# Row 0's mean from two scaled sums, its first weight slice on two queues, and row 1 turned sooner

## The chip, the cores and the metric

One core of one Trainium2 chip. The metric is device microseconds of one execution; the kernel before takes 503.67 us (median of 3 runs, 503.43 to 503.75).

## The reference, cut to what matters

```python
xn = _layernorm(x)                       # x: 1 x 2048 x 576, bf16; eps 1e-5, no scale or shift
return x + _A_ref(xn, A_wqkv, A_wo) + _B_ref(xn, B_w_gate, B_w_up, B_w_down)

# A: dilated local attention, 32 heads of 18, each position looks at 8 keys, 2 apart
qkv = xn @ wqkv                          # 576 -> 1728
logits = einsum(q, k[pos - 2 * w]) * scale, w = 0..7; attn = softmax(logits)
o = einsum(attn, v[pos - 2 * w]) @ wo
# B: SwiGLU, 576 -> 4608 -> 576
(silu(xn @ w_gate) * (xn @ w_up)) @ w_down
```

## The kernel before, in words

The 2048 positions lie as 16 rows of 128: partition p holds positions 16p to 16p + 15, and "row r" is one position of each partition, a tile of 128 x 576. The first 60 us normalize the rows and compute QKV row by row; then four turns of 512 positions follow, each with nine chunks of the gate and up projections (L601) and the down projection (L630), while VectorE computes the attention beside them. The change touches the first 16 us only.

A matmul needs a row with its 576 columns on the partitions, so each normalized row is turned in five slices of 128 columns (the last holds columns 512 to 575 twice, the copy being the "pad"). Rows 0 and 1 are turned on TensorE with 128 x 128 transposes into PSUM (`transp_pe`, L258) and copied to SBUF (`copy_pt`, L267); rows 2 to 4 with half transposes (`transp_halves`, L274), whose two halves ScalarE and VectorE copy (L287); rows 5 and up by DMA transposes. The weights of QKV (576 x 1728) lie as four slices of 128 rows (`load_w`, L147: slices 0 to 3, 432 KB each) and a rest of 64 rows in two DMAs.

Row 0 is treated apart, since everything waits for it. VectorE takes mean and variance (`ln_stats`, two `bn_stats` of 288 columns at L214 and a `bn_aggr` at L218), subtracts the mean only (`ln_center`, L248; GpSimd does the pad, L253), and the centered row is turned and multiplied. Its rstd (`ln_sqrt` on ScalarE, L226, then `ln_recip` on VectorE, L231) is multiplied in where row 0's results leave PSUM (`p_evac`, L345). The fully normalized row 0 (`ln_apply`, L236) is made as well, for the later projections, and turned by a DMA transpose.

The order on every engine is the order of the calls in the program, written by hand (L477 to L551); engines run in order and wait for each other by semaphores that the tile layer places. Ahead of row 0, ten matmuls of 512 columns and one of 128 on constants (`warm_pe`, L171) keep TensorE busy. Then row 0 is turned; QKV row 0 begins with slices 0, 1 and half of 2 (`p_whole`, L304); between its matmuls row 1's transposes stand, in three PSUM tiles (`pt1`, `pa`, `pb`); then slice 0 of row 1, slice 3 and the rest of row 0; then `p_row(1)`, with row 2's half transposes inside it at the place (0, 2), that is, in its second pass behind slice 2 of the first group pair; then `p_row(2)`. PSUM has 8 tiles in rotation: four results of row 0, four of row 1; row 2's half transposes take over the first two of row 0's.

Loads go out on two queues: ScalarE's (x row 0, weight slice 1) and SP's (x row 1, slice 0, slice 2, x row 2, slice 3, the rest, x row 3, then the other 12 rows in three DMAs). Eight DMA semaphores are used in turn, so a DMA's issue waits until the eighth DMA before it has landed.

Of the kernel before, what the change touches and what calls it, by code (L numbers as in the profile page):

```python
# [9 lines left out]
bf16 = mybir.dt.bfloat16  # L10
f32 = mybir.dt.float32
ACT = mybir.ActivationFunctionType
ALU = mybir.AluOpType
# [4 lines left out]
P = 128  # L18
H, DH, W, DIL = 32, 18, 8, 2
D = H * DH  # L20
HALF = D // 2
G = 432
# [3 lines left out]
DPAD = KT * P  # L26
# [44 lines left out]
def kernel(  # L71
# [11 lines left out]
    nc = tc.nc  # L83
# [6 lines left out]
    x_v = A_x.rearrange("b (p r) d -> p (b r) d", r=R)  # L90
    out_v = out.rearrange("b (p r) d -> p (b r) d", r=R)

    const = ctx.enter_context(tc.tile_pool(name="const", bufs=1))
# [19 lines left out]
    PP = big.tile([P, 2, RT * D], bf16, name="PP")  # L113
# [8 lines left out]
    wdf = wd[:].rearrange("p f j -> p (f j)")  # L122
    XC, XN = RT * D, RT * DPAD
    xc_b = [wdf[:, i * XC:(i + 1) * XC].rearrange("p (r d) -> p r d", d=D) for i in range(4)]
# [4 lines left out]
    wqkv = hTf[:, 0:12 * D].rearrange("p (k j) -> p k j", j=3 * D)  # L129
# [14 lines left out]
    def load_x(eng, j):  # L144
        eng.dma_start(xc_b[0][:, j:j + 1, :], x_v[:, j:j + 1, :])

    def load_w(eng, kt):  # L147
        if kt < 4:
            eng.dma_start(wqkv[:, kt, :], A_wqkv[kt * P:(kt + 1) * P, :])
        else:  # L150
            for i in range(2):
                eng.dma_start(wqkvr[64 * i:64 * i + 64, :], A_wqkv[4 * P:D, 2 * G * i:2 * G * (i + 1)])

    load_x(nc.scalar, 0)
    load_x(nc.sync, 1)
    load_w(nc.scalar, 1)
    load_w(nc.sync, 0)
    make_identity(nc, ident[:])
    load_w(nc.sync, 2)
    load_x(nc.sync, 2)  # L160
    load_w(nc.sync, 3)
    load_w(nc.sync, 4)
    load_x(nc.sync, 3)
    for c in range(1, 4):
        nc.sync.dma_start(xc_b[c], x_v[:, 4 * c:4 * c + 4, :])
    nc.scalar.activation(warm[:], eps_t[:], ACT.Sqrt)

    wp = ps.tile([P, 512], f32, name="warm_ps", tag="ps")
    pt1 = wp[:].bitcast(bf16)

    def warm_pe(n, m):  # L171
        one = lambda shape: nc.const_aps.tensor(1.0, shape, bf16)
        for i in range(n):
            nc.tensor.matmul(wp[:].rearrange("p (a b) -> p a b", b=P), one([P, P]), one([P, 4, P]),  # L174
                             start=True, stop=True)
        for i in range(m):
            nc.tensor.matmul(wp[:, 0:P], one([P, P]), one([P, P]), start=True, stop=True)  # L177
# [18 lines left out]
    def new_ps(name):  # L196
        return ps.tile([P, 512], f32, name=name, tag="ps")


    ln = {}  # L200

    def ln_open(c):
        mv = lns.tile([P, 4, 2], f32, name="mv")
        rstd = lns.tile([P, 4], f32, name="rstd")
        ln[c] = (xc_b[c], xn_b[c % 2], mv, rstd)

    sums = {}

    def ln_half(r, k):
        c, j = divmod(r, 4)  # L210
        xc, xn, mv, rstd = ln[c]
        if k == 0:
            sums[r] = lns.tile([P, 2, 6], f32, name="stats")
        nc.vector.bn_stats(sums[r][:, k, :], xc[:, j, k * HALF:(k + 1) * HALF])  # L214

    def ln_aggr(r):
        c, j = divmod(r, 4)
        nc.vector.bn_aggr(ln[c][2][:, j, :], sums[r][:].rearrange("p c s -> p (c s)"))  # L218

    def ln_stats(r, n=1):  # L220
        for i in range(r, r + n):
            ln_half(i, 0)
            ln_half(i, 1)
            ln_aggr(i)

    def ln_sqrt(r, n=1):  # L226
        c, j = divmod(r, 4)
        xc, xn, mv, rstd = ln[c]
        nc.scalar.activation(rstd[:, j:j + n], mv[:, j:j + n, 1], ACT.Sqrt, bias=eps_t[:], scale=1.0)

    def ln_recip(r, n=1):  # L231
        c, j = divmod(r, 4)
        rstd = ln[c][3]
        nc.vector.reciprocal(rstd[:, j:j + n], rstd[:, j:j + n])

    def ln_apply(r):  # L236
        c, j = divmod(r, 4)
        xc, xn, mv, rstd = ln[c]
        dst = xn[:, j] if r else xn0
        nc.vector.tensor_scalar(dst[:, 0:D], xc[:, j], mv[:, j, 0:1], rstd[:, j:j + 1],  # L240
                                op0=ALU.subtract, op1=ALU.mult)
        if r < 2:
            nc.gpsimd.tensor_scalar(dst[:, D:DPAD], xc[:, j, 512:D], mv[:, j, 0:1], rstd[:, j:j + 1],
                                    op0=ALU.subtract, op1=ALU.mult)
        else:
            nc.vector.tensor_copy(dst[:, D:DPAD], dst[:, 512:D])

    def ln_center(r, lo=0, hi=D):  # L248
        c, j = divmod(r, 4)
        xc, xn, mv, rstd = ln[c]  # L250
        nc.vector.tensor_scalar(xn[:, j, lo:hi], xc[:, j, lo:hi], mv[:, j, 0:1], None, op0=ALU.subtract)

    def ln_center_pad(r):  # L253
        c, j = divmod(r, 4)
        xc, xn, mv, rstd = ln[c]
        nc.gpsimd.tensor_scalar(xn[:, j, D:DPAD], xc[:, j, 512:D], mv[:, j, 0:1], None, op0=ALU.subtract)

    def transp_pe(r, kts, pt):  # L258
        c, j = divmod(r, 4)
        xn = ln[c][1]  # L260
        for i, kt in enumerate(kts):
            nc.tensor.transpose(pt[:, i * P:(i + 1) * P], xn[:, j, kt * P:(kt + 1) * P], ident[:])  # L262

    def xT_of(r):
        return xcT if r == 0 else xnT[:, :, r * P:(r + 1) * P]

    def copy_pt(eng, r, kts, pt):  # L267
        eng(xT_of(r)[:, kts[0]:kts[-1] + 1, :],
            pt[:, 0:len(kts) * P].rearrange("p (k t) -> p k t", t=P))

    def new_pt():
        return ps.tile([P, 8 * P], bf16, name="pt", tag="ps")
# [26 lines left out]
    def p_mm(t, g, kt, half, r, start, stop):  # L299
        rows = slice(0, P) if half is None else slice(64 * half, 64 * half + 64)  # L300
        return nc.tensor.matmul(t[g][:, 0:G], xT_of(r)[rows, kt, :], w_at(g, kt, rows),  # L301
                                start=start, stop=stop)

    def p_whole(r, t, kt, gs=range(NG)):  # L304
        for g in gs:
            p_mm(t, g, kt, None, r, kt == 0, False)
# [6 lines left out]
    def fence_after(mm):  # L313
        f = nc.gpsimd.engine_nop()
        tc.add_manual_dep(f.ins, mm.ins.name, SYNC, reason="first half done")
        return f

    def fence_before(mm, f):
        tc.add_manual_dep(mm.ins, f.ins.name, SYNC, reason="banks change row tiles")

    def p_row(r, between=None, at=(0, 1), t=None):


        done = t is not None
        t = t or [None] * NG
        fence = {}
        for swap in range(2):
            for i in range(2):
                for kt in (0, 1, 2, 3) if swap else (0, 4, 1, 2, 3):
                    if done and kt == 0:  # L330
                        continue
                    for half in range(2):
                        g = i + 2 * (half ^ swap)
                        if t[g] is None:
                            t[g] = new_ps("qkv_ps")
                        mm = p_mm(t, g, kt, half, r, swap == 0 and kt == 0, swap == 1 and kt == 3)
                        if swap == 0 and kt == 3 and half == 1:
                            fence[i] = fence_after(mm)
                        if swap and kt == (1 if done else 0) and half == 0:
                            fence_before(mm, fence[i])  # L340
                    if swap and (i, kt) == at and between is not None:
                        between()
        return t
# [130 lines left out]
    def turn(r):  # L474
        return lambda: transp_halves(r)

    warm_pe(10, 1)  # L477
    ln_open(0)
    ln_stats(0)
    ln_center_pad(0)  # L480
    ln_center(0, 0, P)
    ln_sqrt(0)
    pa, pb = new_pt(), new_pt()
    transp_pe(0, (0,), pa)
    ln_center(0, P, D)
    transp_pe(0, range(1, KT), pb)
    copy_pt(nc.scalar.copy, 0, (0,), pa)
    copy_pt(nc.scalar.copy, 0, (1, 2), pb)
    ln_stats(1)
    ln_sqrt(1)  # L490
    copy_pt(nc.scalar.copy, 0, (3, 4), pb[:, 2 * P:])
    ln_recip(0)
    ln_apply(0)
    ln_recip(1)
    ln_apply(1)

    t = [new_ps("qkv_ps") for g in range(NG)]
    p_whole(0, t, 0)
    p_whole(0, t, 1)
    p_whole(0, t, 2, (0, 1))  # L500
    transp_pe(1, (0, 1), pt1)
    transp_pe(1, (2,), pa)
    copy_pt(nc.scalar.copy, 1, (0, 1), pt1)
    copy_pt(nc.vector.tensor_copy, 1, (2,), pa)
    p_whole(0, t, 2, (2, 3))
    transp_pe(1, (3, 4), pb)
    copy_pt(nc.scalar.copy, 1, (3, 4), pb)
    u = [None] * NG
    for g in (0, 2, 1, 3):
        u[g] = new_ps("qkv_ps")  # L510
# [9 lines left out]
    load_gu(0)  # L520
    transp_dma(0)

    p_row(1, turn(2), (0, 2), u)
    ln_aggr(3)
    p_evac(1, u, (0, 1, 2), dve=(1, 2))
    ln_sqrt(3)
# [8 lines left out]
    t = p_row(2, turn(3))  # L535
# [6 lines left out]
    t = p_row(3, turn(4))  # L542
# [10 lines left out]
    for r in range(4, R):  # L553
        t = p_row(r)
# [92 lines left out]
    for tt in range(NTT):  # L647
# [29 lines left out]
        for sub in range(0, RT, 2):  # L677
            t, fence = {}, {}
# [36 lines left out]
```

## Time and profile before

| | before |
|---|---|
| median of 3 runs | 503.67 us |
| the profiled execution | 503.82 us |
| its span | 502.0 us |
| granted TensorE clock, mean | 1.000 |
| TensorE matmul busy | 498.1 us, 99% |
| VectorE, ScalarE, GpSimd busy | 329.0, 200.5, 2.6 us |
| DMA | 75.42 MB, 150 GB/s over the span |
| x row 0 used first | 3.81 us |
| QKV row 0, first matmul | 6.06 us |
| last QKV matmul ends, chunks begin | 60.19 us |

The span is the time between the first and the last instruction on record; the execution's own time has 1.8 us around it. Times in the profile count from the span's start. A row of the time line gives start, busy time, engine, line, operation, output and input, how many instructions are merged, and in brackets how long the engine was idle before them and who ended the wait. "PEld" is TensorE's weight load, which may stand ahead of the matmul that it belongs to.

### The profile page before, as it was taken

How to read it: one execution, taken by the hardware profiler on the slowest of the kernel's cores; microseconds unless marked ns; L12 is line 12 of the kernel's file. 1: busy time of each engine (PE TensorE's matmuls, PEld its weight loads, DVE VectorE, ACT ScalarE, POOL GpSimd, SP SyncE). 2: the span in 40 equal slices, each digit the busy share in tenths (PEclk: the TensorE clock that was granted, in tenths of full speed). 3: DMA queues.
4: the chain of work that ended last, by engine and by line, in shares of the span. 5: the costliest groups of instructions: out<-in, count | busy, mean ns of one | idle time of the engine just before them, and what ended most of it. 6: DMA issues, size and time to landing. Idle time of an engine off the chain costs nothing.

```text
span 502.0 us, 13267 instructions
## 1 busy us (share of the span) xinstructions
PE 498.1 (99%) x5795; PEld 330.5 (66%) x5795; DVE 329.0 (66%) x478; ACT 200.5 (40%) x415; POOL 2.6 (1%) x9
## 2 busy tenths in 40 slices
PE   9999999999999999999999999999999999999997
PEld 4666655555799755555899655555999555557996
DVE  5888598898999698999898139995980222221001
ACT  4756657644400255554300445557000454553000
POOL 2000000000000000000000000000000000000000
PEclk9999999999999999999999999999999999999999
DMA  8889988789921045536621154465600335453100
GB/s 313 219 206 228 307 280 280 220 273 309 233 82 61 25 136 193 191 106 225 161 69 43 29 185 146 139 189 157 136 25 14 100 114 178 155 177 38 29 14 25
DMA packets 77186, 75.42 MB, mean 150 GB/s; under 512 B 22708, under 2 KB 72528, under 8 KB 77128
## 3 DMA queue, kind: packets, MB, share of 16 engines
q1 hardware_dynamic: 76840, 73.98, 49.7%
q8 instruction: 45, 0.74, 0.6%
q10 hardware_dynamic: 288, 0.59, 0.4%
q14 instruction: 13, 0.11, 0.1%
HBM read 58.76 MB, written 5.90 MB: 129 GB/s over the span
## 4 chain that ended last, share of the span: by engine, by line
PE 99%; DVE 0%; issue 0%
PE g_ps L601 56%; PE d_ps L630 32%; PE qkv_ps L301 11%; PE warm_ps L174 1%; PE pt L262 0%; DVE ot L644 0%; PE pt L283 0%; PE warm_ps L262 0%; PE warm_ps L177 0%
## 5 line engine op out<-in xcount | busy, mean ns | idle before, releaser
L601 PE MATMUL g_ps<-xnT,gu 64*128 64x512 bf16 x2592 | 280.4, 376 | 0.0
L601 PEld LDWEIGHTS <-gu 64*128 64x128 bf16 x2592 | 147.7, 94 | 131.3
L612 ACT ACTIVATE sg<-g_ps 128x512 bf16<-128x512 f32 x144 | 87.3, 606 | 156.6 <-PE g_ps L601 156.6
L630 PE MATMUL d_ps<-wd,hT 64*128 64x288 bf16 x2304 | 146.9, 283 | 0.0
L630 PEld LDWEIGHTS <-hT 64*128 64x128 bf16 x2304 | 131.3, 94 | 10.5
L614 DVE TENSOR_TENSOR hT<-sg,uc 128x512 bf16<-128x512 bf16 x144 | 60.0, 418 | 93.8 <-ACT uc L613 93.6
L613 ACT CAST uc<-g_ps 128x512 bf16<-128x512 f32 x144 | 85.2, 592 | 0.0
L414 DVE TENSOR_REDUCE PP<-PP 128x64 f32<-128x1152 bf16 x64 | 84.9, 1345 | 0.4
L301 PE MATMUL qkv_ps<-hT,xnT 64*128 64x432 bf16 (+1 forms) x536 | 50.2, 343 | 0.0
L409 DVE TENSOR_TENSOR PP<-QO,Kr 128x2304 bf16<-128x2304 bf16 (+1 forms) x35 | 43.5, 1249 | 7.2 <-DMA Kr<-hT 6.9
L642 DVE TENSOR_TENSOR ot<-d_ps,xr 128x288 bf16<-128x288 f32 x30 | 12.3, 451 | 51.1 <-PE d_ps L630 51.1
L441 DVE TENSOR_TENSOR PP<-Vr,A 128x2304 bf16<-128x2304 bf16 (+1 forms) x35 | 43.2, 1250 | 0.4
L301 PEld LDWEIGHTS <-xnT 64*128 64x128 bf16 (+1 forms) x536 | 30.1, 94 | 18.5 <-ACT xnT L287 0.4
L446 DVE TENSOR_TENSOR PP<-PP 128x2304 bf16<-128x2304 bf16 x24 | 32.5, 1353 | 0.3
L612 ACT ACT_TABLE_LOAD x5 | 6.4, 1283 | 47.3 <-PE g_ps L601 47.2
L630 PE MATMUL d_ps<-wo,xnT 64*128 64x288 bf16 x288 | 23.4, 283 | 0.0
L363 ACT CAST hT<-qkv_ps 128x288 bf16<-128x288 f32 (+2 forms) x58 | 21.2, 428 | 0.5 <-DMA kv_d<-hT 0.5
L630 PEld LDWEIGHTS <-xnT 64*128 64x128 bf16 x288 | 16.4, 94 | 1.2
L434 ACT ACTIVATE PP<-PP 128x1024 f32<-128x1024 f32 x4 | 4.2, 1057 | 31.2 <-DVE PP L430 31.2
L644 ACT CAST ot<-d_ps 128x288 bf16<-128x288 f32 x1 | 0.4, 399 | 38.8 <-PE d_ps L630 38.8
L363 ACT CAST QO<-qkv_ps 128x432 bf16<-128x432 f32 (+1 forms) x30 | 12.3, 410 | 7.4 <-PE qkv_ps L301 7.4
L214 DVE BATCH_NORM_STATS2 stats<-wd 128x6 f32<-128x288 bf16 x32 | 12.9, 444 | 2.9 <-DMA wd<-in_A_x_dram 2.6
(53 smaller groups left out, 91.3 us busy)
## 6 DMA issues: line engine op xcount, KB each, us to landing
gu<-in_B_w_gate_dram SPq DMA_DIRECT2D x36, 512.0 KB, 3.8
gu<-in_B_w_up_dram SPq DMA_DIRECT2D x36, 512.0 KB, 5.1
wd<-in_B_w_down_dram SPq DMA_DIRECT2D x9, 576.0 KB, 6.0
kv_d<-hT SPq DMA_DIRECT2D x5, 576.0 KB, 6.4
gu<-in_B_w_gate_dram SPq DMA_DIRECT2D x36, 64.0 KB, 4.7
gu<-in_B_w_up_dram SPq DMA_DIRECT2D x36, 64.0 KB, 4.4
xr<-in_A_x_dram SPq DMA_DIRECT2D x8, 288.0 KB, 5.1
out_dram<-ot SPq DMA_DIRECT2D x16, 144.0 KB, 1.8
```

The costliest lines, as they stand in the source:

```text
L214: nc.vector.bn_stats(sums[r][:, k, :], xc[:, j, k * HALF:(k + 1) * HALF])
L301: return nc.tensor.matmul(t[g][:, 0:G], xT_of(r)[rows, kt, :], w_at(g, kt, rows), start=start, stop=stop)
L363: (nc.vector.tensor_copy if n in dve else nc.scalar.copy)(*parts[n])
L409: nc.vector.tensor_tensor(prod[:, a:b], QO[:, RT * tt + a:RT * tt + b, :], Kr[:, s:s + b - a, :], op=ALU.mult)
L414: nc.vector.tensor_reduce(L[:, w, rs], prod[:, rs].rearrange("p r (h d) -> p r h d", d=DH), axis=AX.X, op=ALU.add)
L441: nc.vector.tensor_tensor(dst[:, a:b], Vr[:, s:s + b - a, :].rearrange("p r (d h) -> p r d h", h=H), A[:, w, a:b].unsqueeze(2).to_broadcas ...
L446: nc.vector.tensor_tensor(dst, acc, pv, op=ALU.add)
L601: mm = nc.tensor.matmul(ring_ps[j][b][:], gu[rows, slot, k, fc], xnT[rows, kt, tok], start=(swap == 0 and kt == 0), stop=(swap == 1 and kt ...
L612: nc.scalar.activation(sg[:], t[0][:], ACT.Silu)
L613: nc.scalar.copy(uc[:], t[1][:])
L614: nc.vector.tensor_tensor(hT[:, ch * FC + j, :], sg[:], uc[:], op=ALU.mult)
L630: mm = nc.tensor.matmul(t[sub][h][:, 0:HALF], a[rows], w[rows, h * HALF:(h + 1) * HALF], start=(swap == 0 and n == 0), stop=(swap == 1 and ...
```

## The change

Five edits, all in the first stage:

- Row 0's mean: ScalarE scales columns 0 to 287 by 1/576 and sums them, VectorE does the same for columns 288 to 575; both sums go to `part`, and centering subtracts the two one after the other, with two per-partition scalars. Row 0's `bn_stats` and `bn_aggr`, now only for its rstd, come later, between row 1's.
- Weight slice 0 is loaded in two halves of 864 columns, one on each queue. Slice 1 moves from ScalarE's queue to SP's, behind slice 0's half.
- The last 8 rows of x come in one DMA instead of two.
- One warm-up matmul of 512 columns less.
- Row 1's transposes use `pb` alone and stand two matmuls sooner for the first three, behind slice 1 of row 0; their copies are all ScalarE's (128, 256 and 256 columns). Row 0's square root, reciprocal and full normalizing move behind them. Row 2's half transposes stand one pair of matmuls sooner, at (0, 1).

```diff
     load_x(nc.scalar, 0)
     load_x(nc.sync, 1)
-    load_w(nc.scalar, 1)
-    load_w(nc.sync, 0)
+    for eng, cols in ((nc.scalar, slice(2 * G, 4 * G)), (nc.sync, slice(0, 2 * G))):
+        eng.dma_start(wqkv[:, 0, cols], A_wqkv[0:P, cols])
+    load_w(nc.sync, 1)
     make_identity(nc, ident[:])
...
-    for c in range(1, 4):
-        nc.sync.dma_start(xc_b[c], x_v[:, 4 * c:4 * c + 4, :])
+    nc.sync.dma_start(xc_b[1], x_v[:, 4:8, :])
+    nc.sync.dma_start(wdf[:, 2 * XC:4 * XC].rearrange("p (r d) -> p r d", d=D), x_v[:, 8:16, :])
...
+    part = const.tile([P, 2], f32, name="part")
+
+    def ln_mean0():
+        xc = ln[0][0]
+        nc.scalar.activation(PP[:, 1, 0:HALF], xc[:, 0, 0:HALF], ACT.Copy, scale=1.0 / D, accum_out=part[:, 0:1])
+        nc.vector.tensor_scalar(PP[:, 1, HALF:D], xc[:, 0, HALF:D], 1.0 / D, None,
+                                op0=ALU.mult, op1=ALU.add, accum_out=part[:, 1:2])
...
-        nc.vector.tensor_scalar(xn[:, j, lo:hi], xc[:, j, lo:hi], mv[:, j, 0:1], None, op0=ALU.subtract)
+        nc.vector.tensor_scalar(xn[:, j, lo:hi], xc[:, j, lo:hi], part[:, 0:1], part[:, 1:2],
+                                op0=ALU.subtract, op1=ALU.subtract)
...
-    warm_pe(10, 1)
+    warm_pe(9, 1)
     ln_open(0)
-    ln_stats(0)
+    ln_mean0()
     ln_center_pad(0)
     ln_center(0, 0, P)
-    ln_sqrt(0)
     pa, pb = new_pt(), new_pt()
     transp_pe(0, (0,), pa)
     ln_center(0, P, D)
     transp_pe(0, range(1, KT), pb)
     copy_pt(nc.scalar.copy, 0, (0,), pa)
     copy_pt(nc.scalar.copy, 0, (1, 2), pb)
+    copy_pt(nc.scalar.copy, 0, (3, 4), pb[:, 2 * P:])
     ln_stats(1)
     ln_sqrt(1)
-    copy_pt(nc.scalar.copy, 0, (3, 4), pb[:, 2 * P:])
-    ln_recip(0)
-    ln_apply(0)
+    ln_half(0, 0)
     ln_recip(1)
     ln_apply(1)
+    ln_half(0, 1)
+    ln_aggr(0)
 
     t = [new_ps("qkv_ps") for g in range(NG)]
     p_whole(0, t, 0)
     p_whole(0, t, 1)
-    p_whole(0, t, 2, (0, 1))
-    transp_pe(1, (0, 1), pt1)
-    transp_pe(1, (2,), pa)
-    copy_pt(nc.scalar.copy, 1, (0, 1), pt1)
-    copy_pt(nc.vector.tensor_copy, 1, (2,), pa)
-    p_whole(0, t, 2, (2, 3))
-    transp_pe(1, (3, 4), pb)
-    copy_pt(nc.scalar.copy, 1, (3, 4), pb)
+    transp_pe(1, (0, 1, 2), pb)
+    copy_pt(nc.scalar.copy, 1, (0,), pb)
+    copy_pt(nc.scalar.copy, 1, (1, 2), pb[:, P:])
+    p_whole(0, t, 2, (0, 1, 2))
+    transp_pe(1, (3, 4), pb[:, 3 * P:])
+    copy_pt(nc.scalar.copy, 1, (3, 4), pb[:, 3 * P:])
+    p_whole(0, t, 2, (3,))
+    ln_sqrt(0)
+    ln_recip(0)
+    ln_apply(0)
...
-    p_row(1, turn(2), (0, 2), u)
+    p_row(1, turn(2), (0, 1), u)
```

More of the change, by code (lines that the diff above doesn't have):

```diff
@@ L163 @@
     load_x(nc.sync, 3)
-    for c in range(1, 4):
-        nc.sync.dma_start(xc_b[c], x_v[:, 4 * c:4 * c + 4, :])
+    nc.sync.dma_start(xc_b[1], x_v[:, 4:8, :])
+    nc.sync.dma_start(wdf[:, 2 * XC:4 * XC].rearrange("p (r d) -> p r d", d=D), x_v[:, 8:16, :])
     nc.scalar.activation(warm[:], eps_t[:], ACT.Sqrt)
     wp = ps.tile([P, 512], f32, name="warm_ps", tag="ps")
-    pt1 = wp[:].bitcast(bf16)
     def warm_pe(n, m):
@@ L255, in ln_center_pad @@
         xc, xn, mv, rstd = ln[c]
-        nc.gpsimd.tensor_scalar(xn[:, j, D:DPAD], xc[:, j, 512:D], mv[:, j, 0:1], None, op0=ALU.subtract)
+        nc.gpsimd.tensor_scalar(xn[:, j, D:DPAD], xc[:, j, 512:D], part[:, 0:1], part[:, 1:2],
+                                op0=ALU.subtract, op1=ALU.subtract)
     def transp_pe(r, kts, pt):
```

## The prediction

> **What bounds the kernel now.** I read the chain that ended last in order of time first, then DVE, ACT and PE over the first 17 us, then narrow windows for single starts.
>
> ```profile
> 0.76 4.42 PE warm_ps L174 x10
> ...
> 6.13 2.25 PE qkv_ps L301 x10
> ...
> 9.02 3.86 PE qkv_ps L301 x32
> 12.88 0.15 PE pt L283 x10
> 13.03 3.07 PE qkv_ps L301 x32
> ```
>
> The chain is TensorE from 0.76 us to 498.94, with no gap worth naming. So the time is the start of QKV row 0 plus a fixed amount of matmul work: what an edit in the first 15 us takes off PE's start is won for good, and what it lets PE wait there is lost for good. Ten matmuls of 0.18 should take 1.83, not 2.25; narrow windows give their starts as 6.06, 6.37, 6.73, 6.93, 7.12, 7.30. The first two are 0.31 and 0.36 apart, the rest 0.18 to 0.20: up to about 6.73 PE runs at half rate (the warm-up matmuls, 512 columns in 0.43, are slow too).
>
> ```profile
> 3.81 0.82 DVE L214 BATCH_NORM_STATS2 stats<-wd 128x6 f32<-128x288 bf16 x2 [2.63 <-DMA wd<-in_A_x_dram]
> 4.66 0.21 DVE L218 BATCH_NORM_AGGREGATE mv<-stats 128x2 f32<-128x12 f32 x1
> 4.90 0.56 DVE L251 TENSOR_SCALAR wd<-wd,mv 128x128 bf16<-128x128 bf16 x2
> ...
> 8.58 0.23 DVE L268 COPY xnT<-pt 128x128 bf16<-128x128 bf16 x1 [1.11 <-PE pt L262]
> 8.72 0.81 DVE L214 BATCH_NORM_STATS2 stats<-wd 128x6 f32<-128x288 bf16 x2
> 9.56 0.21 DVE L218 BATCH_NORM_AGGREGATE mv<-stats 128x2 f32<-128x12 f32 x1
> 10.14 0.16 DVE L234 RECIPROCAL rstd<-rstd 128x1 f32<-128x1 f32 x1 [0.36 <-ACT rstd L229]
> 10.34 0.43 DVE L240 TENSOR_SCALAR wd<-wd,mv,rstd 128x576 bf16<-128x576 bf16 x1
> 10.80 0.18 DVE L246 COPY wd<-wd 128x64 bf16<-128x64 bf16 x1
> 11.12 0.94 DVE L365 TENSOR_SCALAR hT<-qkv_ps,rstd 128x432 bf16<-128x432 f32 x2
> 11.98 0.81 DVE L214 BATCH_NORM_STATS2 stats<-wd 128x6 f32<-128x288 bf16 x2
> 13.09 0.49 DVE L287 CAST xnT<-pt 128x320 bf16<-128x320 f32 x1 [0.30 <-PE pt L283]
> ```
>
> Columns: start, busy, engine and line, then in brackets the idle time before and what ended it. Two paths cross here. The first is row 0's: x lands (3.81), sums, mean, centering (4.90), transposes (5.21), copies, first matmul (6.06). The second is DVE's from 8.72 on: it normalizes row 2, evacuates row 0, and at 13.09 copies half of row 2's transposes. Row 2's matmuls need that copy:
>
> ```profile
> 13.70 0.14 PEld L301 LDWEIGHTS <-xnT 64*128 64x128 bf16 x4 [0.37 <-ACT xnT L287]
> ```
>
> The first weights of row 2 load at 13.70, 0.12 behind the end of DVE's copy (13.58; ACT's half ended at 13.49), and their matmul starts at 13.73, where 13.60 was due. So the second path already ends at PE. Its slack is what DVE idled: 0.30 ahead of the copy and 0.22 ahead of 11.12 (the copy of 10.80 frees DVE at 10.90).
>
> **The change, part by part.** *Mean of row 0.* Removed from the path: two sums and their aggregate, 3.81 to 4.90, 1.09. Added: one scaled sum of 288 columns on ACT and one on DVE, side by side, each with an accumulator output that no row shows. ACT's nearest row reads SBUF at L434: 1024 elements in 1.057; slope from ACT's PSUM copies (512 in 0.59, 256 in 0.37: 0.86 ns each), so 288 take 0.42 to 0.44. DVE's nearest is the sum at L214, 0.45. Not below 0.35 (a copy of 256), and with a further small instruction to write the accumulator (nearest: ACT's 128x1 at 0.20 to 0.29; DVE's reciprocal at 0.11 to 0.16) not above 0.75. Centering then waits for both engines. I take 0.65 from landing to centering, so it starts at 4.5 instead of 4.90; ends 4.25 and 4.75. GpSimd's pad (0.58) starts with it and gains a second scalar (0.64 to 0.74 at L243); it feeds the fifth transpose only. One warm-up matmul (0.43) goes, so PE is free at about 4.75, just ahead of the first transpose at 4.81. First matmul: 6.06 less 0.40, 5.66.
>
> *Half rate.* If the rate changes at 6.73 again, three matmuls run slow instead of two and the eighth ends at 7.65; before it ended at 7.85. So 0.40 at the front is worth 0.20.
> The Trainium skill, "TensorE: Matmul & The Clock Gate", Part 1, says that the clock rises once a free-running window of about 3.4 us was busy, wherever the kernel starts in it. That this chip took 5.97 us from PE's start agrees with a window that began late; in another execution the rate may change sooner, and the whole 0.40 would count at the front.
> I work out that case too (next part).
>
> *Slice 0 in halves, slice 1 to SP.* Slice 0 now has 0.74 MB to finish with it instead of 1.18 (rows 0 and 1, slices 0 and 1); at 0.41 MB per us, as at 5 to 6 us, it lands 1.1 sooner, near 4.9, ahead of 5.66. Slice 1 has the same bytes ahead of it and lands near 5.7 as before (SP's issue at 5.76 waited for it); it is wanted at 6.9. Slice 2 (7.15), 3 (9.1) and 4 keep their bytes and their uses; each SP issue behind slice 1 comes 0.46 later, and the queue is backed up by more than that. The merged x load and the shifted slot waits touch data used after 14 us. Row 0's DMA transpose now waits for a normalizing that ends at 10.2 and for GpSimd's pad of it, some 0.74 behind that start; SP came to it at 11.61. Zero.
>
> *Row 1.* Its transposes stand two matmuls sooner, and all five use one PSUM tile. In the built program the fourth transpose waits for ScalarE's second copy of row 1, since that copy reads the same tile. With S the first transpose: third at S+0.11, first copy S+0.36 (0.25 behind, as 8.27 to 8.52 before), second copy S+0.57 to S+0.94, fourth transpose S+0.99, where three matmuls alone would have it at S+0.72. S is 7.65 (row 1's normalizing is no later: behind centering its sums start at +0.49, the aggregate at +1.33, ACT's root at +1.86 behind row 0's copies, the reciprocal at +2.19, normalizing from +2.39 to +2.82, which is 7.32). So row 1's first QKV matmul comes at S+1.27 = 8.92; before it came at 8.95. The front gain is spent here: 0.03 is left.
>
> *Row 0's rstd behind row 1's copies.* ScalarE's square root now stands behind row 1's last copy: copy S+1.30 to 1.67, root to S+1.90. VectorE, in order, waits at the reciprocal: S+1.94 = 9.59, normalizing row 0 at 9.79, and **row 2's sums start at 10.13 instead of 8.72**. What DVE did for row 0 at 6.35 to 6.93 and for row 1 at 8.58 stood in idle time; now it stands ahead of row 2. From there by the rows' own distances: aggregate 10.97, reciprocal 11.55, normalize 11.75, pad 12.21, evacuation 12.31 and 12.90, row 3's sums 13.17, copy of row 2's transposes 13.90 to 14.39. ScalarE's evacuation of row 0 waits behind row 2's root (11.22) and holds one transpose bank of row 2 to 12.7; that one is turned one matmul pair sooner but ends near 12.9, hidden behind what follows.
>
> *Sum.* Row 2's matmuls start 0.15 behind that copy, at 14.54 instead of 13.73: **+0.81**, with PE idle for 0.7 ahead of them. DVE has 0.34 idle ahead of the next copy (16.29), so the lag does not grow; nothing later gives PE time back. The profiled execution of 503.82 (span 502.0) would be 504.63; it lies 0.15 over the median of the runs, so 503.67 becomes 504.48. With centering at 4.25, S is 7.55 at least (+0.71); at 4.75, 7.78 (+0.94). With an early full rate S is 7.41, but the kernel before would gain 0.34 in that case too: +0.57 if only the new run is early, +0.91 if both.
>
> **Rivals.** *The front gain stays* (13%): DVE's path is hidden after all, because row 2's normalizing or the copy is quicker than these distances. Then 0.03 to 0.40 is won: 503.3 to 503.6. For it: DVE has 1.1 us idle at 7.5 to 8.6. Against: that idle time lies before the reciprocal's wait, and row 2's copy was late already.
> *The sums cost what they replace* (18%): the two accumulators with their reads take 1.1 us, centering stays at 4.90 or later, S is 7.85 to 7.95 and row 2 starts at 14.74 to 14.84: 504.7 to 504.8, slower by over 0.2%. It decides from a centering start of 4.9 on. For it: no row has an accumulator.
> *PE's new idle time lowers its rate* (4%): 0.25 at row 1 and 0.7 at row 2, then one 3.4 us stretch at half rate: +1.7, 506.2. Nothing in the trace shows a gap of that size, so it can't be excluded.
> *The change nets nothing* (10%): ScalarE's second copy is not waited for and the root comes 0.3 sooner: 503.7 to 504.0.
>
> **How the numbers follow.** My forecast has 55%: +0.81, 504.5, its own range 504.1 to 504.9. The range 503.5 to 505.2 leaves out the rate drop and most of the first rival, and allows for row distances that add up wrong by some tenths. About 0.2%, 1.0 us, is what a measurement can tell from no change. Faster by that can't come from a front that moves 0.4: 2%. Slower by it: the second and third rival (22%) and the upper part of my own (a fifth of 55%, with 1.0 against 0.81): 33%. The rest, 65%, is within it, on the slower side.
>
> **What would show it.** Right: the fourth transpose of row 1 waits for ACT's copy near 8.6; DVE's reciprocal at 9.6 waits for ACT; row 2's sums at 10.1; PE's weights for row 2 idle until 14.5. Wrong: row 2's first weights near 13.5, or centering at 4.9.

## The result, and the profile after

The changed kernel takes 505.47 us (median of 7 runs, 504.52 to 505.95) against 503.67 (7 runs, 503.36 to 504.20): a ratio of 1.003, 95% interval 1.002 to 1.004, or 1.8 us more. The forecast of 504.5 had the sign and not quite half of the amount; 505.47 is 0.27 over the upper end of the range, and on the slower side of the 0.2% bound, which had a chance of 33%.

The profiled execution took 505.52, span 503.7. First TensorE's row 0 to row 2 on the time line of after (start, busy time, engine and line, in brackets the idle time before and who ended it):

```profile
4.93 0.92 PE L271 MATMUL pt<-ident,wd 128*128 128x128 bf16 x5
5.63 1.26 PE L310 MATMUL qkv_ps<-hT,PP 128*128 128x432 bf16 x4
7.08 0.89 PE L310 MATMUL qkv_ps<-hT,PP 128*128 128x432 bf16 x4 [0.18 <-DMA hT<-in_A_wqkv_dram]
7.80 0.33 PE L271 MATMUL pt<-ident,wd 128*128 128x128 bf16 x3
8.20 0.71 PE L310 MATMUL qkv_ps<-hT,PP 128*128 128x432 bf16 x3
8.76 0.27 PE L271 MATMUL pt<-ident,wd 128*128 128x128 bf16 x2
...
10.46 1.36 PE L310 MATMUL qkv_ps<-hT,PP 128*128 128x432 bf16 x8 [0.51 <-DMA hT<-in_A_wqkv_dram]
```

The reader is to see two things. The front came as planned: the first QKV matmul at 5.63 instead of 6.06. And two new waits stand behind it, both for weight slices (`hT<-in_A_wqkv_dram`): slice 1 at 7.08, slice 3 at 10.46, where the kernel before used slice 3 at 9.69 without waiting. (Slice 2 is late too: the chain has it landing just ahead of the matmuls at 8.20.)

The other path, VectorE and ScalarE of after:

```profile
3.97 0.45 DVE L213 TENSOR_SCALAR_CACHE_REDUCE PP<-wd 128x288 bf16<-128x288 bf16 x1 [2.77 <-DMA wd<-in_A_x_dram]
4.35 0.08 DVE L213 DVE_READ_ACCUMULATOR PP<-wd 128x1 f32 x1
4.56 0.62 DVE L258 TENSOR_SCALAR wd<-wd,part 128x128 bf16<-128x128 bf16 x2
...
9.67 0.16 DVE L241 RECIPROCAL rstd<-rstd 128x1 f32<-128x1 f32 x1 [1.67 <-ACT rstd L236]
...
10.21 0.81 DVE L221 BATCH_NORM_STATS2 stats<-wd 128x6 f32<-128x288 bf16 x2
...
13.97 0.47 DVE L296 CAST xnT<-pt 128x320 bf16<-128x320 f32 x1
```

```profile
3.97 0.44 ACT L212 ACTIVATE PP<-wd 128x288 bf16<-128x288 bf16 x1 [0.81 <-DMA wd<-in_A_x_dram]
4.32 0.18 ACT L212 ACTIVATION_READ_ACCUMULATOR PP<-wd 128x1 f32 x1
```

The two sums with their accumulator reads take 0.59 from landing to centering (3.97 to 4.56). VectorE then stands idle for 1.67 ahead of row 0's reciprocal, and row 2's sums start at 10.21. Row 2's first weights load at 14.56; the profile puts their wait of 0.47 down to ScalarE's copy, but that had ended at 14.18, and VectorE's copy (13.97 to 14.44) ends 0.12 ahead of them, the same 0.12 as in the kernel before.

Behind the first stage the chain of after, which was TensorE alone before, leaves TensorE once more:

```profile
131.28 4.54 DMA xnT<-QO
...
135.86 35.45 PE d_ps L641 x576
```

Those are the DMA transposes of the attention's output that the first down projection needs; TensorE's matmuls wait 0.5 for them there, its weight load 0.8.

| us | before | after | lag |
|---|---|---|---|
| first QKV matmul | 6.06 | 5.63 | -0.43 |
| first with slice 1 (the fifth) | 7.12 | 7.08 | -0.04 |
| row 1's first | 8.95 | 9.05 | +0.10 |
| slice 3's first | 9.69 | 10.46 | +0.77 |
| row 2's first | 13.73 | 14.61 | +0.88 |
| QKV ends, chunks begin | 60.19 | 61.05 | +0.86 |
| first down projection, first `wo` matmul | 134.35 | 135.86 | +1.51 |
| TensorE's last result taken over | 498.94 | 500.46 | +1.52 |
| span | 502.0 | 503.7 | +1.7 |

So the loss has three parts: 0.86 in the first 15 us, which the forecast had at 0.81; 0.65 at the first down projection, for which it had no term; and 0.2 behind the last instruction.

### The profile page after: what moved, and what is told of

The parts are those of the page before. It is cut to its first block, busy times and chain, and to the rows that moved or that the text cites. A ratio compares the mean times of both kernels' runs of the same rounds, so it can differ in the third digit from the quotient of the medians.

```text
span 503.7 us, 13269 instructions
## 1 busy us (share of the span) xinstructions
PE 498.3 (99%) x5794; PEld 294.9 (59%) x5794; DVE 329.2 (65%) x479; ACT 201.2 (40%) x418; POOL 2.8 (1%) x9
## 4 chain that ended last, share of the span: by engine, by line
PE 94%; DMA 2%; DVE 2%; ACT 1%; issue 1%; SPq 0%
PE g_ps L612 54%; PE d_ps L641 31%; PE qkv_ps L310 9%; DMA hT<-in_A_wqkv_dram 1%; DMA xnT<-QO 1%; DVE PP L423 1%; DVE PP L418 0%; DVE hT L374 0%; DVE hT L625 0%; DVE stats L221 0%; ACT uc L624 0%; ACT rstd L236 0%; ACT hT L376 0%; DVE ot L655 0%; DVE wd L247 0%
## 5 line engine op out<-in xcount | busy, mean ns | idle before, releaser
L612 PEld LDWEIGHTS <-gu 64*128 64x128 bf16 x2592 | 132.4, 94 | 146.7
L641 PEld LDWEIGHTS <-hT 64*128 64x128 bf16 x2304 | 113.6, 94 | 28.3
L641 PEld LDWEIGHTS <-xnT 64*128 64x128 bf16 x288 | 14.0, 94 | 4.2 <-DMA xnT<-QO 0.8
```

What stands on the lines that cost most here:

```text
L612: mm = nc.tensor.matmul(ring_ps[j][b][:], gu[rows, slot, k, fc], xnT[rows, kt, tok], start=(swap == 0 and kt == 0), stop=(swap == 1 and kt ...
L641: mm = nc.tensor.matmul(t[sub][h][:, 0:HALF], a[rows], w[rows, h * HALF:(h + 1) * HALF], start=(swap == 0 and n == 0), stop=(swap == 1 and ...
```

## The experiments

Each ratio is against the kernel before on the same chip: 503.6 (503.3 to 504.32) beside e1 to e4, 503.73 (503.18 to 506.06) beside f1 to f4, 503.86 (503.31 to 505.02) beside r1, r2, h1 and h2. "Lag" is a point of TensorE's time line against the profiled execution of before. Every time line is that of one execution, and medians and time lines need not agree.

### The two halves of the front: loads and VectorE's order

Two theories for the 0.86. A: VectorE's order, the reciprocal that waits at 9.67 (the forecast's step). B: the loads, which the forecast priced at zero.

**e1**: the changed kernel with slices 0 and 1 loaded as before (the merged load of x stays).

```diff
-    for eng, cols in ((nc.scalar, slice(2 * G, 4 * G)), (nc.sync, slice(0, 2 * G))):
-        eng.dma_start(wqkv[:, 0, cols], A_wqkv[0:P, cols])
-    load_w(nc.sync, 1)
+    load_w(nc.scalar, 1)
+    load_w(nc.sync, 0)
```

> The changed kernel with the loads of slices 0 and 1 as before (slice 0 whole on SP, slice 1 on ScalarE's queue). Theory A (VectorE's order alone holds row 2): slice 3's matmuls go back to near 9.7 us, but row 2's first weights still load near 14.5, QKV ends near 61.0 instead of 60.2, and the time stays 0.8 or more over before: 504.5. Rival B (the weight slices land later and hold TensorE): the waits at 7.1, 8.2 and 10.5 go, QKV ends near 60.2 to 60.4 and the time is within 0.3 of before.

Measured: 504.5 (504.35 to 505.38, 11 runs), ratio 1.0018 [1.001, 1.0027]. The first matmul comes at 5.87 (it waits 0.31 for slice 0), row 1's transposes at 7.33, and row 2's matmuls wait again behind VectorE's path:

```profile
14.11 1.09 PE L309 MATMUL qkv_ps<-hT,xnT 64*128 64x432 bf16 x10 [0.55 <-ACT QO L371]
```

QKV ends 0.38 late. From the first transpose of row 1 to row 2's matmuls it is 6.78 here (7.33 to 14.11) and 6.81 in after (7.80 to 14.61): theory A's distance is fixed. Row 1's transposes come 0.47 later in after. Not all of that is the loads: e1's first QKV matmuls ran at full rate, those of after in part at half. In f1 below, which has the front of after and the full rate, they come at 7.64, 0.31 behind e1.

**e2**: the changed kernel with row 0's reciprocal moved behind row 2's root, and row 0's full normalizing and DMA transpose to row 7.

```diff
     ln_sqrt(0)
-    ln_recip(0)
-    ln_apply(0)
...
     ln_sqrt(2)
+    ln_recip(0)
     normalize(2)
...
     load_gu(0)
-    transp_dma(0)
...
     normalize(7)
+    ln_apply(0)
+    transp_dma(0)
```

> The changed kernel with row 0's reciprocal put just ahead of row 2's normalizing, and row 0's full normalizing with its DMA transpose behind row 7's: VectorE starts row 2's sums near 8.1 instead of 10.2. Theory A: row 2's first weights load near 13.7, QKV ends near 60.2, the time is 503.6 to 504.2 (the upper end if the first down projection still waits for its DMA transposes). Rival B: slice 3's matmuls still start near 10.4, TensorE is 0.7 late from there on, QKV ends near 60.9.

Measured: 505.5 (504.89 to 507.56, 6 runs), 1.0046 [1.0032, 1.006]. Row 2's sums start at 8.43, where VectorE waits 0.72 for x of row 2 and no longer for the root; the slices still come late (waits of 0.55 ahead of slice 1, 0.38 ahead of slice 3), and the lag at row 3's transposes is +0.35 (16.44 against 16.09). The place chosen for row 0's DMA transpose was a bad one: on SP's queue it pushes those of rows 8 to 11 back (the chain names 5.38 us of `xnT<-wd` from 35.87), which costs 0.63 more. The time says nothing on A or B for that reason; the time line up to 17 us does.

**e3**: both edits, **e1**'s and **e2**'s.

> Both edits: loads of slices 0 and 1 as before, and row 0's rstd out of row 2's way. Theories A and B together: no wait at 10.5 and none at row 2, QKV ends at 60.0 to 60.2, 503.4 to 503.7. If it is still over 504.2, a third cost (row 1's transposes in one tile, the merged x load, or the wait of the first down projection) is larger than both.

Measured: 505.01 (504.88 to 505.68, 5 runs), 1.0032 [1.002, 1.0044]. Row 2's weights load at 13.15 instead of 13.70, and at the transposes of row 4 TensorE is 0.52 ahead of before. At the end of QKV 0.20 of that is left; **e2**'s misplaced DMA transpose is the likely taker of the rest. The first down projection then loses 0.98, and 1.1 more goes behind TensorE's last result; so the expected 503.4 to 503.7 is missed by over a microsecond, for reasons behind the front.

**e4**: the loads edits alone (halves, slice 1 on SP, merged load of x) in the kernel before.

> The kernel before with only the loads changed (slice 0 in halves, slice 1 on SP's queue, the last 8 rows of x in one DMA). Theory A: nothing in front of row 2 hangs on it, 503.7, as before. Rival B: slice 1 lands near 7.0 instead of 5.7 and slice 3 near 10.4 instead of 9.1; TensorE waits at slice 1 or slice 3, QKV ends 0.5 to 0.9 later, 504.2 to 504.6.

Measured: 505.46 (504.99 to 506.64, 5 runs), 1.0045 [1.0032, 1.0058]: alone they cost as much as the whole change, and more than theory B's 0.5 to 0.9. From the time line of e4:

```profile
7.32 0.89 PE L302 MATMUL qkv_ps<-hT,PP 128*128 128x432 bf16 x4 [0.23 <-DMA hT<-in_A_wqkv_dram]
8.43 0.52 PE L302 MATMUL qkv_ps<-hT,PP 128*128 128x432 bf16 x2 [0.22 <-DMA hT<-in_A_wqkv_dram]
...
10.88 1.36 PE L302 MATMUL qkv_ps<-hT,PP 128*128 128x432 bf16 x8 [0.45 <-DMA hT<-in_A_wqkv_dram]
```

Every slice behind the first is waited for, and QKV ends 1.19 late. Why is in the table of windows; its last column is what the DMA engines moved in the microsecond from 5 to 6, in before and then in e4:

```profile
5.00:6.00 1.00, 0.98 (x7) 0.55 (x6) 1.00 (x4) 0.46 (x2) 0.55 (x1) 1.00 1.06 429
```

```profile
5.00:6.00 1.00, 1.00 (x8) 0.63 (x7) 1.00 (x4) 0.31 (x2) 0.40 (x1) 1.00 1.01 200
```

The engines are shown busy in both (1.06 and 1.01) and move half as much in e4. By 8 us, before has loaded 2.28 MB and e4 1.95; 0.33 MB at 0.4 MB per us is about 0.8 us. (The merged load of x, part of this edit, was not run alone; e1 has it and waits for no slice behind slice 0.)

**f4**: what e3 should have been: e1's and e2's edits, but row 0's normalizing and DMA transpose ahead of rows 4 and 5, where both engines idle, and x in three loads again.

```diff
     ln_sqrt(4, 2)
     p_evac(2, t, (3, 4, 5), dve=())
+    ln_apply(0)
+    transp_dma(0)
     normalize(4, 2)
```

> The changed kernel with the loads as before (slice 0 whole on SP, slice 1 on ScalarE's queue, x in three DMAs), row 0's reciprocal just ahead of row 2's normalizing, and row 0's full normalizing and DMA transpose where both engines idle (VectorE ahead of rows 4 and 5, SP at 17 us). What stays of the change: the mean from two sums, row 1's order, row 2's turn one pair sooner. If the two costs (loads, VectorE's order) are all that the front lost, row 2's matmuls start 0.5 us sooner than before (13.2), no DMA transpose of rows 5 to 11 is late, QKV ends at about 59.7, and the time is 503.1 to 503.3 if the first down projection does not wait. If it waits as in the other variants, 0.5 to 1.0 comes on top: 503.6 to 504.2.

Measured: 504.57 (503.7 to 505.34, 11 runs), 1.0013 [1.0004, 1.0022]. No wait is left on TensorE's matmuls behind slice 0's; row 2's weights load at 13.02 instead of 13.70, QKV ends 0.65 and TensorE 0.63 sooner than before. So in the time lines A and B together are all that the front lost, as expected; the time of 503.1 to 503.3 that was to follow did not come:

| lag of TensorE, us | loads as before | loads changed |
|---|---|---|
| row 0's reciprocal ahead of row 2's normalizing | -0.63 (f4) | +0.35 (e2, at row 3) |
| row 0's reciprocal as changed | +0.38 (e1) | +0.86 (after) |

Each cost is about 1.0 alone; together they are less than the sum, since a row 2 that is late for the one reason waits less for the other.

The entries are single executions, and TensorE's change from half to full rate shifts them. f4, e1, e2 and f1 have the full rate from the first QKV matmul on, before and after have not. With f1 in the place of after, +0.71 stands for +0.86, and all four entries are alike in this. Against before they flatter the change: h2 below, which differs from the kernel before by one warm-up matmul and also has the early full rate, turns row 2 at 12.20 (before 12.72), and f4 at 12.04. Like against like the best front gains 0.16 there; r1, f4's kernel with a late full rate, gains 0.31 against before at the same place, and its TensorE ends 0.26 sooner.

### Halves or queue

**f2**: the kernel before with slice 0 in halves, slice 1 left on ScalarE's queue behind its half. **f3**: the kernel before with slices 0 and 1 whole, both on SP.

```diff
-    load_w(nc.scalar, 1)
-    load_w(nc.sync, 0)
+    load_w(nc.sync, 0)
+    load_w(nc.sync, 1)
```

> The kernel before with slice 0 in column halves on the two queues, but slice 1 left on ScalarE's queue behind its half. Tells the two parts of the loads edit apart. Theory 'one queue': what costs 1.19 us of QKV in the run with all of the loads edit is that ScalarE's queue is empty from 4.1 us on; with slice 1 on it, 5 to 6 us moves near 400 GB/s as before, slices 2 and 3 are used at about 7.2 and 9.3 to 9.7, and QKV ends within 0.3 of 60.19. Rival 'halves': the half rows of 1.7 KB go slower than whole rows of 3.5 KB; then the rate at 5 to 6 us is near 200 GB/s, slice 3 is waited for beyond 10, and QKV ends 0.6 or more late.

> The kernel before with slices 0 and 1 whole, one behind the other, both on SP's queue; the counterpart of the run before. Theory 'one queue': ScalarE's queue is done with x row 0 by about 3.8, SP's alone moves some 200 to 330 GB/s, slice 0 is waited for at 6 or later and slice 3 beyond 10.3; QKV ends 0.8 to 1.6 late, 504.5 to 505.5. Rival 'halves': whole rows are as quick on one queue as on two, and QKV ends within 0.3 of 60.19.

f3: 504.86 (504.37 to 505.9, 8 runs), 1.002 [1.0009, 1.003]; QKV 0.42 late, between the 0.8 to 1.6 of theory "one queue" and the 0.3 of its rival. But f3 has the early full rate; against h2, which has it too, row 2 is turned 0.94 later (13.14 against 12.20). Whole rows did not help; the rate falls as in e4:

```profile
5.00:6.00 1.00, 0.84 (x8) 0.36 (x7) 0.96 (x5) 0.56 (x2) 0.58 (x1) 1.00 0.88 211
```

f2: 505.05 (503.88 to 506.79, 9 runs), 1.0026 [1.0011, 1.0041], although its trace keeps 404 GB/s in that microsecond and ends QKV 0.13 early (again with the early full rate: row 2 is turned 0.39 behind h2's). That execution was the quickest of the nine, so the kernel was run once more.

> The run f2_halves_two_queues once more: its trace (503.88) was the quickest of nine runs, the median 505.05. The trace shows slice 1 waited for at 6.99 (0.46) and QKV ending 0.13 sooner than before. Theory 'rate': a trace of 504.9 or more shows half rate beyond 6.8. Rival 'halves': such a trace shows slices landing later than in the first one, with TensorE waiting for a weight slice by 1 us or more. Rival 'transposes': QKV ends in time, and the first down projection waits.

Measured: 506.36 (505.15 to 509.11, 7 runs), 1.0054 [1.0033, 1.0074]. The profiled execution took 507.63, and it shows two things that no other one had. Time line, then windows (the column ahead of the last two is TensorE's granted clock):

```profile
8.45 2.15 PE L302 MATMUL qkv_ps<-hT,PP 128*128 128x432 bf16 x6 [1.81 <-DMA hT<-in_A_wqkv_dram]
```

```profile
7.00:8.00 1.00, 0.00 (x0) 0.00 (x0) 0.35 (x1) 0.00 (x0) 0.80 (x2) 1.00 1.01 395
8.00:9.00 1.00, 0.55 (x3) 0.25 (x3) 0.00 (x0) 0.00 (x0) 0.00 (x0) 0.83 1.13 284
9.00:10.00 1.00, 1.00 (x4) 0.41 (x3) 0.00 (x0) 0.00 (x0) 0.00 (x0) 0.50 1.08 317
...
12.00:13.00 1.00, 1.00 (x7) 0.56 (x6) 0.60 (x3) 0.48 (x2) 0.00 (x0) 0.97 1.00 401
```

Slice 1 was used at 6.99 in f2 and at 8.45 here: the last 0.03 MB on ScalarE's queue trickle in (0.02 MB between 6 and 7 us, 0.01 between 7 and 8) while SP's queue moves 0.35 and 0.38; why they come so late was not tested. And TensorE, idle for 1.81, fell to half its clock 0.2 us after it resumed. 0.83 means 0.34 us of half clock before 9, then three full microseconds, then 0.06 (0.97): 3.4 us at half rate, or 1.7 lost. That is one execution; no other trace has an idle time of this length behind the warm-up.

What is shown: in all five traces with slice 1 on SP's queue (after, e2, e4, f1, f3) the loads move 200 to 287 GB/s between 5 and 6 us, in the others, with it on ScalarE's, 384 to 429; f3 differs from before in that alone. Halving slice 0 costs by another way: slice 1, behind its half on ScalarE's queue, came at 7.0 in one execution and at 8.4 in the other. Why SP's queue alone is slow just there is open: from 6 to 8 us before runs on it alone as well, at 379 and 391.

The Trainium skill, "DMA: Bandwidth & Descriptors", section "Issuing engines are not separate DMA queues", says that starting transfers from several engines saves only the time of issuing them. Here the measurement differs: the issues were all out in time, and with one queue the same engines moved 0.3 MB less by 8 us.

### The first down projection

**f1**: the changed kernel with the residual's loads of x behind the DMA transposes that the first down projection waits for.

```diff
-            if ch == 7:
+            if ch == NCH - 1:
                 for i in (0, 2):
                     nc.sync.dma_start(xr[:, i:i + 2, :], x_v[:, RT * tt + i:RT * tt + i + 2, :])
```

> The changed kernel with one edit far from it: in each turn the two loads of x for the residual (xr) stand behind the four DMA transposes that the first down projection waits for, not ahead of them. If the first down projection is late because SP holds its transposes behind those loads, SP issues them at about 130 us as in the kernel before, the wait of 0.5 at 135.4 goes, and the time is 504.6 to 505.0 (505.47 less 0.5 to 0.9). If the transposes are late because all 16 DMA engines are taken there, the wait stays and the time is 505.3 to 505.6. The QKV lag of +0.86 stays in both cases.

Measured: 505.1 (504.7 to 505.97, 8 runs), 1.0029 [1.0019, 1.004]. That lies between the two ranges. Its trace has no wait at the first down projection. For the transposes (L670) the profile gives the time from issue to landing, in after and then in f1:

```profile
DMA to landing us min/median/max: 2.7/3.0/4.5
```

```profile
DMA to landing us min/median/max: 2.6/2.6/2.7
```

The transposes can be issued when the last chunk ends (in the kernel before SP waits for its last matmul), and there the first `wo` matmul stands 4.23 behind that point. What is lost there is what issue and flight of the first transpose take over 4.2:

| us | issued behind the chunks' end | first transpose in flight | lost |
|---|---|---|---|
| before | 0.03 | 3.4 | 0 |
| f1 | 0.03 | 2.6 | 0 |
| f2 | 0.62 | 3.4 | 0 |
| f3 | 0.93 | 3.4 | 0.12 |
| after | 0.30 | 4.5 | 0.65 |
| e1 | 0.99 | 4.1 | 0.91 |
| e3 | 1.40 | 3.8 | 0.98 |
| r2, the same kernel as f2 | 0.03 | 4.9 | 0.71 |

So the kernel before had a slack of 0.8 there. SP's loads of x at L685 wait until an earlier load of `gu` lands (1.5 us in after), and the transposes stand behind them; that is the first column, and only 0.27 of after's loss. The rest is the longer flight. In f1, with the loads of x out of the way, no transpose takes over 2.7, which fits transfers that run beside them, but it is one execution. Nor does the loss follow from TensorE's lag: e4 comes to this place 1.19 late and loses nothing, e3 comes 0.20 early and loses 0.98, and f2 and r2 are one kernel. What makes the flight long in one execution and not in another is open, and so is how much of the 0.65 belongs to the change. The worth of f1's edit can't be told from the times either: 505.1 against 505.47, from separate sets of runs and with overlapping intervals.

### Does TensorE's idle time cost clock, and where f4's gain went

f4's trace ends 0.63 sooner on TensorE, its median 0.8 later than before. Theory "rate": in other executions the small idle times at 4.5 to 5.8 postpone the full rate.

> The run f4_best_front once more: its profiled execution took 503.7, the median of its runs 504.57, and the trace of 503.7 shows nothing that would cost the difference. Over all traces so far TensorE's change from half to full rate falls anywhere from 3.9 to 6.7 us. Theory 'rate': in executions where the change comes late, TensorE's idle 0.2 to 0.6 us at 4.5 to 5.8, which the kernel before does not have, postpones it further, at half of that time. Then the median is 504.2 to 504.8 again, and a trace that falls into the upper part shows QKV matmuls of 0.35 instead of 0.18 beyond 6.8. Rival 'chip': the chip of the second set was a restless one (the kernel before spread to 506.06 there); then the median here is 503.0 to 503.4. Rival 'transposes': an upper trace shows the first down projection waiting for its DMA transposes.

> The run f4_best_front with TensorE kept busy in its gaps: the tenth warm-up matmul of 512 columns back, and three of 128 columns between row 0's transposes and its first QKV matmul. The first QKV matmul comes up to 0.3 later (near 6.0). Theory 'rate': the median falls below f4's in spite of it, to 503.2 to 503.7, and the runs spread as little as the kernel before's on the same chip. Rivals: no change but the later start, 504.5 to 504.9 if f4 repeats at 504.6.

> The kernel before with nine warm-up matmuls of 512 columns instead of ten, nothing else: TensorE idles 0.4 us ahead of row 0's transposes, which start no sooner and no later (they wait for centering, 5.2). Theory 'rate': the median rises by 0.3 to 1.2 and the spread with it, although no instruction of the path has moved. Rival: the same as before within 0.2.

The edits of h1 (to f4) and h2 (to the kernel before):

```diff
-    warm_pe(9, 1)
+    warm_pe(10, 1)
...
+    warm_pe(0, 3)
     p_whole(0, t, 0)
```

```diff
-    warm_pe(10, 1)
+    warm_pe(9, 1)
```

r1 took 504.38 (503.9 to 506.31, 12 runs), 1.0013 [1.0004, 1.0022]; h1 504.28 (503.97 to 504.97, 11 runs), 1.001 [1.0002, 1.0019]; h2 503.8 (503.45 to 505.15, 11 runs), 1.0001 [0.9993, 1.001]. h2's gap:

```profile
5.27 0.71 PE L262 MATMUL pt<-ident,wd 128*128 128x128 bf16 x5 [0.66 <-DVE wd L251]
```

A gap of 0.66 in the kernel before costs nothing, so the theory falls for gaps of this size. h1 says less than was planned: it closes the gap ahead of row 0's transposes, but slice 0 comes late and still leaves 0.49 ahead of the first QKV matmul; its median is that of r1. "Chip" falls too: f4 repeats.

The traces show another cause. Behind the last instruction, the last output has to land. DMA view of f4 from 498.8 to 502.5 us (queue, packets, MB, share of the 16 engines; then KB and us to landing):

```profile
q14 instruction: 1, 0.01, 1.0%
...
out_dram<-ot SPq DMA_DIRECT2D x1, 144.0 KB, 2.2
```

The first line is a load of instructions, one packet that holds one DMA engine for 0.6 us (1.0% of 16 engines over 3.7). In before it comes past the end of the span, and the same output lands in 1.7. Over all fourteen traces the pattern is the same. In f4, r1, e2, h1 and e3 the packet falls beside the last output, takes 0.6, 0.6, 0.6, 0.7 and 0.8, and the output lands in 2.2, 2.3, 2.3, 2.5 and 2.7; in the other nine it comes past the end and the output lands in 1.7. The output is late by about the time that the packet takes. These five are the programs with row 0's reciprocal moved. From VectorE's last result to the end of the span it is 2.6 in before, 3.1 in f4, 3.2 in r1, 3.4 in h1 and 3.7 in e3.

So the profiled executions close. r1: TensorE's end 0.26 sooner, the tail 0.56 longer, the span 0.3 longer (502.3 against 502.0); h1: 0.41 sooner, 0.8 longer, 0.4 longer. Their medians, 0.5 and 0.4 over before's, leave 0.2 and almost nothing open. f4's profiled execution, 503.7, was the quickest of its eleven, and for its median most of the 0.8 stays open. That the packet makes the landing late is an inference from these pairs; no run took it away. No version of the change beats the kernel before.

## Where the prediction was right and where wrong, point by point

- *Mean of row 0*: right. Centering 0.59 behind the landing of x (0.65 was taken), the first matmul at 5.63 (5.66).
- *Half rate*: right in kind. Two of the first four matmuls ran at half rate (starts 5.63, 6.00, 6.36, 6.54), where three were forecast. Over the traces the full rate comes at very different times (f4's first eight matmuls take 1.62, r1's, the same kernel, 2.04).
- *Row 1*: right in size. The fourth transpose stands 0.96 behind the first (0.99). In after two things end together ahead of it, ScalarE's second copy (8.71) and the matmuls behind the late slice 2; in e1, where slice 2 is not late, the distance is 0.96 too.
- *Row 0's rstd*: right in mechanism and size. Reciprocal 9.67 (9.59), row 2's sums 10.21 (10.13), VectorE's copy 13.97 (13.90), row 2's matmuls 14.61 (14.54).
- *The loads, "Zero"*: this step failed. It counted the bytes ahead of each slice and took 0.41 MB per us for all of them, a rate from the kernel before with slice 1 on the other queue. The changed kernel moved 259 GB/s from 5 to 6 us, and slice 1, forecast to land near 5.7, held TensorE until 7.08. Alone the edit costs 1.19 at the end of QKV and 1.9 in the median. In the sum it hid: the forecast had row 1's first transpose at 7.65 because of half rate, it came at 7.80 because of slice 1, and VectorE's path from there is so long that most of TensorE's wait for slice 3 lies beside it. So +0.81 came out near +0.86 partly by luck: in e1, with the loads of before and the full rate from its first QKV matmul on, row 1's transposes came at 7.33 and the lag was 0.38.
- *"Nothing later gives PE time back"*: true, but the sum ended with the front, and a missing term is the second step that failed. It had none for the first down projection, where 0.65 more was lost in the profiled execution, nor for the 0.2 behind the last instruction. In the kernel before that spot has no wait, and its slack of 0.8 was not worked out; the range reached 505.2 for distances that add up wrong, and 505.47 lies beyond it.
- *Rivals.* The sums did not cost what they replace. TensorE's rate did not fall in after (1.00 in each microsecond from 3 to 15 us), but r2 has such a drop behind an idle time of 1.81, with the price of 1.7 that was named. "The front gain stays" needs both the loads and the reciprocal undone (f4, -0.63; r1, -0.26), and then the end takes it.

## What to carry to other kernels

A load moved to another queue is no zero because its bytes are the same: price it by the rate that the remaining queue has alone, in the window in which it must land, and bound it by the slack of every user. A sum that ends with its stage has to be followed to every place where a transfer is only just in time, and to the landing of the last output; the slack of such a place is worth working out beforehand. One trace is one execution: where the median of a variant lies half a microsecond beyond its profiled execution, take a second trace before the first is believed, and compare only traces whose TensorE came to full rate at the same time.

## What the runs showed of the hardware

- An accumulator output is a second instruction: 0.18 on ScalarE (`ACTIVATION_READ_ACCUMULATOR`), 0.08 on VectorE (`DVE_READ_ACCUMULATOR`).
- After 1.81 us idle TensorE ran at half its clock for 3.4 us (r2, one execution); after 0.66 it did not (h2). The Trainium skill, "TensorE: Matmul & The Clock Gate", Part 1, gives at least one idle window of about 3.4 us as the condition. The 3.4 us of half rate agree with its window; here the drop came after an idle time of about half a window.
- In the warm-up the profile's granted clock reads 1.00 while 512 columns take 0.43 us; from 9 to 12 us of r2 it reads 0.50 while 432 columns take 0.36. The column shows the second slowdown, not the first.
- A load of instructions beside the last output goes with a landing in 2.2 to 2.7 us instead of 1.7 (five traces against nine); the packet takes 0.6 to 0.8 us of one DMA engine.
